# The second matrix product of the last pair of token tiles, by seven block products instead of eight

## The chip, the core and the metric

The kernel runs on one core of a Trainium2 chip. TensorE multiplies matrices into PSUM banks; VectorE and ScalarE do element-wise work; GpSimd has no part in what follows; SyncE (SP) issues the DMAs that move data between HBM and SBUF. Each engine works through its own queue in order and waits on semaphores. The metric is the device time of one execution in microseconds; lower is better.

## What is computed

```python
scores = scale * np.matmul(q, k.transpose(0, 1, 3, 2))     # 8 batches, 8 heads, 576 tokens, 64 dims
scores = np.where(masks[None], scores, -1e9)               # window 32, or 32 keys at a dilation of 4
attn = softmax(scores)
x = np.matmul(attn, v) -> (4608, 512)
h = x @ w_in                                               # (4608, 2048)
g = np.maximum(h, 0.0) + alpha * np.minimum(h, 0.0)
out = g @ w_out                                            # (4608, 512)
```

All in float32. On TensorE a float32 number is kept as two parts, a high one (a cast) and a low one (the number less its cast), and a product is three matmul passes: high by high, high weight by low data, low weight by high data (`PASSES`).

## The kernel before

There are 9 tiles of 512 tokens. The first three are worked one by one, mixed with most of the attention. Tiles 3 to 8 are worked as three pairs: (3, 4), (5, 6), (7, 8), in `paired_stage`. For each pair the hidden layer of 2048 is taken in two groups (`grp` 0 and 1) of four units; a unit is 256 hidden rows, two blocks of 128. Each group has two stages: `phase_h` (first product and activation) and `phase_y` (second product).

In `phase_h` the first product of a unit is already done by seven block products in place of eight (Strassen's scheme in Winograd's form). They are numbered 1 to 7, each is six matmuls of 512 columns, and their order for a unit is 1, then 3 and 4 of the unit before, then 7, 6, 2, 5. Bank A takes 1, 6, 5, 3 and is copied out after 1, 6 and 5 (`snap`, ScalarE, L646); banks B and C take 2, and 7 and 4, and are added to the copies (`add`, VectorE, L653). The four blocks of the hidden layer are called 11, 12, 21, 22: the first digit is the block of hidden rows, the second the token tile. For each, `negative` takes relu(-h) (ScalarE, L660), `value` builds the activation (VectorE, L664), `high` casts (ScalarE, L668) and `low` subtracts (VectorE, L672).

`phase_y` does the second product plainly: for each of four blocks `c` of 128 output features, eight blocks `j` of hidden rows, two token tiles and three passes, 192 matmuls (L742). Group 0 copies its sums to `partial` (L760, L762); group 1 adds them and stores the result (L765). Its steps are counted 8c + j, and `hooks` puts other work into all engines' queues at a step: the remaining attention pairs (five in the first stage, three, four and none in the next three; `scores`, `maxima`, `exponentials`, `divisions`, `turns`, `values`) and the splitting of the next pair's tokens (`token_parts`, L583 to L589). The last pair has neither.

The weights come back from HBM scratch (`wS`: seven blocks a unit for the first product, sums included; `wO`: plain split blocks for the second) through a ring of ten slots of 256 KB: `take` uses one, `feed` puts the next load on SP's queue. The buffers g1 to g4 hold the snapshots of `phase_h` and are free in `phase_y`.

The order of all instructions is written by hand; each engine's queue has them in program order.

Of the kernel before, what the change touches and what calls it, by code (L numbers as in the profile page):

```python
# [8 lines left out]
F32 = mybir.dt.float32  # L9
F32R = mybir.dt.float32r  # L10
# [7 lines left out]
P = 128  # L18
# [6 lines left out]
BK = 2 * BQ  # L25
# [35 lines left out]
def tile_window_attention_prelu_ffn(  # L61
# [31 lines left out]
    part = dram.tile([NC, P, TT], F32, name="part")  # L93
    wS = dram.tile([NFP, 7, P, 2, 2 * P], F32, name="wS")
    wO = dram.tile([NF // GF, NC, GP, P, 2, 2, P], F32, name="wO")

    turn = {"a": 0, "y": 0, "g": 0}

# [376 lines left out]


    WBLOCK = {1: 0, 2: 1, 4: 2, 3: 3, 7: 4, 5: 5, 6: 6}

    def save(f):

# [41 lines left out]
    PRODUCTS = (1, 7, 6, 2, 5, 3, 4)  # L522
    STEPS = [(i, q) for i in range(NFP) for q in PRODUCTS]
    units = []
    for _ in range(NSTD, NTILE, 2):
        for grp in range(NFP // GP):
            seq = []
            for i in range(GP):
                seq.append((i, 1))
                if i:  # L530
                    seq += [(i - 1, 3), (i - 1, 4)]
                seq += [(i, 7), (i, 6), (i, 2), (i, 5)]
            second = [wO[grp, c, j].rearrange("p f a n -> p (f a n)") for c in range(NC) for j in range(GP)]
            units += [wS[grp * GP + i, WBLOCK[q]].rearrange("p a n -> p (a n)") for i, q in seq]
            units.append(second[0])
            units += [wS[grp * GP + GP - 1, WBLOCK[q]].rearrange("p a n -> p (a n)") for q in (3, 4)]
            units += second[1:]
# [11 lines left out]

    def feed():  # L550
        if fed[0] < len(units):
            nc.sync.dma_start(out=slot(fed[0]).bitcast(F32), in_=units[fed[0]])
            fed[0] += 1

    def take():
# [120 lines left out]
            return gpart(2 * self.i + n // 20, n % 2 == 0)  # L676

    ABANKS = [f"a{i}" for i in range(4)]

    def third(u):  # L680
        u.mm(3)
# [15 lines left out]
        u.value(11)  # L697
        u.value(22)

    def phase_h(t, grp):  # L700

        last = None
        for i in range(GP):
            u = Four(t, grp, i)
            u.mm(1)
            u.snap(1)
            if last:
                after_first(last)
                third(last)
                fourth(last)  # L710
            u.mm(7)
            if last:
                last.low(22)
                last.low(12)
            u.mm(6)
            u.snap(2)
            if last:
                last.high(21)
            u.mm(2)
            u.add(11)  # L720
            if last:
                last.low(21)
            u.mm(5)
            u.snap(3)
            u.negative(11)
            u.add(22)
            last = u
        return last

    def phase_y(t, grp, u, hooks):  # L730

# [35 lines left out]
        for op in hooks.get(GF * NC, ()):  # L767
            op()

    def attention_hooks(hooks, us, start, step):  # L770
        def put(n, *ops):
            hooks.setdefault(min(n, GF * NC), []).extend(ops)
# [28 lines left out]
    def paired_stage():  # L801
# [4 lines left out]
        for t in range(NSTD, NTILE, 2):  # L806
            for grp in range(NFP // GP):
                hooks = {}
                last = phase_h(t, grp)
                if t == NSTD:  # L810
                    us, todo = (todo[:5], todo[5:]) if grp == 0 else (todo[:3], todo[3:])
                else:
                    us, todo = (todo[:4], todo[4:]) if grp == 0 else ([], todo)
                if us:
                    attention_hooks(hooks, us, *{5: (2, 5), 4: (3, 6), 3: (3, 5)}[len(us)])
                if grp and t + 2 < NTILE:
                    lots = token_parts(t + 2)
                    for at, lot in zip((7, 16, 22) if t == NSTD else (5, 11, 14), lots):
                        for k, op in enumerate(lot):
                            hooks.setdefault(at + k, []).append(op)  # L820
                phase_y(t, grp, last, hooks)

    late_ops = {}
# [321 lines left out]
```

## Time and profile before

| what | us |
|---|---|
| median of 3 runs | 876.26 |
| lowest and highest | 875.46, 878.27 |
| the profiled execution, its own time | 875.48 |
| span of the profiled execution, first to last instruction | 873.4 |
| TensorE busy in it | 845.0 |
| VectorE busy | 536.2 |
| ScalarE busy | 404.9 |

The span is what the profile's views divide up. In the rows, PE is TensorE, PEld its weight loads, DVE VectorE, ACT ScalarE, POOL GpSimd and SPq the DMA queue of SyncE; L742 is line 742 of the kernel; `out<-in` are the program's names for what an instruction writes and reads; "idle before <-X" is how long the engine stood before an instruction, and what ended the wait. [...]

### The profile page before, as it was taken

The numbers are of one execution on the slowest core, as the hardware profiler recorded it, in microseconds if no ns is written. First come the engines' busy times: TensorE is split into PE (matmuls) and PEld (weight loads), VectorE is DVE, ScalarE is ACT, GpSimd is POOL, SyncE is SP. The second block draws the span as 40 slices with busy tenths as digits, with TensorE's granted clock in tenths as the row PEclk, the third lists the DMA queues.
The fourth block names the chain that finished last, engine by engine and source line by source line (L and its number), as shares of the span: only waits on it lengthen the run. The fifth ranks groups of instructions, "written<-read, shape, count | busy, mean of one in ns | idle before, by whom it ended". The sixth has DMA issues, their size and how long they took to land.

```text
span 873.4 us, 19846 instructions
## 1 busy us (share of the span) xinstructions
PE 845.0 (97%) x8144; PEld 695.3 (80%) x8144; DVE 536.2 (61%) x924; ACT 404.9 (46%) x1153; POOL 46.9 (5%) x52
## 2 busy tenths in 40 slices
PE   4789999999999999999999999999999999999998
PEld 3577888888888788887788888887888888888886
DVE  5988767676776768675537665764277537304721
ACT  6785766534334344555436533643264226204500
POOL 0000000200505340000000000000000000000000
PEclk9789999999999999999999999999999999999999
DMA  9723344136889964765657666655475466336641
GB/s 337 250 72 121 121 163 145 41 103 203 275 283 317 283 211 127 254 184 162 186 166 193 186 178 192 193 153 157 127 193 151 150 188 192 114 96 178 183 122 48
DMA packets 95449, 152.81 MB, mean 175 GB/s; under 512 B 8448, under 2 KB 39168, under 8 KB 95360
## 3 DMA queue, kind: packets, MB, share of 16 engines
q1 hardware_dynamic: 95360, 151.55, 57.4%
q8 instruction: 64, 1.05, 0.5%
q14 instruction: 25, 0.20, 0.1%
HBM read 117.96 MB, written 33.55 MB: 173 GB/s over the span
## 4 chain that ended last, share of the span: by engine, by line
PE 95%; ACT 1%; issue 1%; DVE 1%; DMA 1%; SPq 0%
PE y L742 31%; PE h L406 16%; PE y L454 15%; PE pA L604 15%; PE pC L604 7%; PE pB L604 4%; PE o L279 3%; PE s L199 2%; PE o L230 1%; PE s L212 1%; DMA ws<-w_in 1%; ACT w_dt.float L249 1%; ACT wa L376 0%; ACT wa L375 0%; DVE x L338 0%
## 5 line engine op out<-in xcount | busy, mean ns | idle before, releaser
L406 PE MATMUL h<-x,w_dt.float32r 128*128 128x512 f32 x576 | 144.5, 400 | 2.9 <-issue 1.4
L454 PE MATMUL y<-g,w_dt.float32r 128*128 128x512 f32 x576 | 138.3, 389 | 0.0
L406 PEld LDWEIGHTS h<-x,w_dt.float32r 128*128 128x128 f32 x576 | 109.0, 192 | 26.9 <-issue 1.8
L454 PEld LDWEIGHTS y<-g,w_dt.float32r 128*128 128x128 f32 x576 | 107.9, 188 | 22.5
L742 PE MATMUL y<-gp,ring_w 128*128 128x512 f32 x480 | 113.6, 391 | 0.0
L249 ACT ACTIVATE pr<-pr,nm 128x64 f32<-128x64 f32 x216 | 72.2, 336 | 76.6 <-DVE nm L242 76.6
L742 PE MATMUL y<-gp,ring_xA 128*128 128x512 f32 x444 | 104.8, 391 | 0.0
L742 PEld LDWEIGHTS y<-gp,ring_w 128*128 128x128 f32 x480 | 89.4, 188 | 18.7
L742 PEld LDWEIGHTS y<-gp,ring_xA 128*128 128x128 f32 x444 | 82.7, 188 | 17.6
L646 ACT COPY stage<-pA 128x512 f32<-128x512 f32 x72 | 42.4, 589 | 105.0 <-PE pA L604 105.0
L432 ACT CAST g<-m 128x512 fp32r<-128x512 f32 x48 | 29.7, 619 | 75.6 <-DVE m L427 72.5
L672 DVE TENSOR_TENSOR gp<-n,gp 128x512 fp32r<-128x512 f32 x96 | 63.2, 684 | 0.0
L664 DVE SCALAR_TENSOR_TENSOR n<-n,bal,stage 128x512 f32<-128x512 f32 x72 | 53.9, 749 | 13.9 <-ACT n L660 13.1
L604 PE MATMUL pA<-parts_w,ring_w 128*128 128x512 f32 x234 | 57.6, 389 | 0.0
L668 ACT CAST gp<-n 128x512 fp32r<-128x512 f32 x96 | 56.6, 615 | 1.8 <-DVE n L664 1.8
L604 PE MATMUL pA<-parts_w,ring_xA 128*128 128x512 f32 x228 | 56.1, 389 | 0.0
L742 PE MATMUL y<-gp,ring_g 128*128 128x512 f32 x228 | 55.0, 393 | 0.0
L660 ACT ACTIVATE n<-stage 128x512 f32<-128x512 f32 x72 | 45.6, 634 | 12.5 <-DVE stage L653 12.0
L604 PEld LDWEIGHTS pA<-parts_w,ring_w 128*128 128x128 f32 x234 | 43.9, 188 | 9.1
L765 DVE TENSOR_TENSOR ob<-y,py 128x512 f32<-128x512 f32 x24 | 16.3, 689 | 54.9 <-PE y L742 54.9
L604 PEld LDWEIGHTS pA<-parts_w,ring_xA 128*128 128x128 f32 x228 | 42.8, 188 | 8.9
L742 PEld LDWEIGHTS y<-gp,ring_g 128*128 128x128 f32 x228 | 42.3, 188 | 9.0
(98 smaller groups left out, 1116.7 us busy)
## 6 DMA issues: line engine op xcount, KB each, us to landing
ring_w<-wS SPq DMA_DIRECT2D x68, 256.0 KB, 2.8
ring_xA<-wS SPq DMA_DIRECT2D x67, 256.0 KB, 2.8
ring_w<-wO SPq DMA_DIRECT2D x40, 256.0 KB, 2.9
ring_xA<-wO SPq DMA_DIRECT2D x37, 256.0 KB, 2.8
out<-ob SPq DMA_DIRECT2D x36, 256.0 KB, 2.9
ring_g<-wS SPq DMA_DIRECT2D x33, 256.0 KB, 3.0
wO<-w_dt.float32r SPq DMA_DIRECT2D x32, 256.0 KB, 4.8
wS<-wc SPq DMA_DIRECT2D x16, 512.0 KB, 3.9
```

The source lines that it names most:

```text
L249: nc.scalar.activation(out=self.pr[:, r, :], in_=self.pr[:, r, :], func=AF.Exp, bias=self.nm[:, r:r + 1], scale=1.0, accum_out=self.sm[:, ...
L279: nc.tensor.matmul(self.po[u][e * D:(e + 1) * D, a:z, :], lhsT=self.v[rows, i, :], rhs=self.pt[rows, a * BK + (BQ if i else 0):z * BK - (B ...
L406: nc.tensor.matmul(ms[t, f], lhsT=weight(0, a, f)[:, c * P:(c + 1) * P], rhs=half(t, c)[:, e, :], start=(c == 0 and n == 0), stop=(c == NC ...
L432: nc.scalar.copy(out=g[:, 0, :], in_=ms[t, f])
L454: nc.tensor.matmul(ys[t][c], lhsT=weight(1, a, f)[:, c * P:(c + 1) * P], rhs=g[:, e, :], start=(first and n == 0), stop=(last and n == 2),)
L604: nc.tensor.matmul(to, lhsT=w[:, (2 * a + c) * P:(2 * a + c + 1) * P], rhs=part_of(name, e)[:, c * TT:(c + 1) * TT], start=start and c == ...
L646: nc.scalar.copy(out=self.s(n), in_=self.A)
L660: nc.scalar.activation(out=self.m[n], in_=self.at(n), func=AF.Relu, scale=-1.0)
L664: nc.vector.scalar_tensor_tensor(out=self.m[n], in0=self.m[n], scalar=bal[:, f:f + 1], in1=self.at(n), op0=ALU.mult, op1=ALU.add)
L668: nc.scalar.copy(out=self.g(n)[:, 0], in_=self.m[n])
L672: nc.vector.tensor_tensor(out=g[:, 1], in0=self.m.pop(n), in1=g[:, 0].bitcast(F32), op=ALU.subtract)
L742: nc.tensor.matmul(ys2[tt], lhsT=w[:, k * P:(k + 1) * P], rhs=g[:, e], start=j == 0 and n == 0, stop=j == GF - 1 and n == 2)
```

## The change

The second product of the last pair is done by seven block products a unit too. A unit's hidden blocks 11, 12, 21, 22 are combined on VectorE to T1 = 12 - 11, T3 = 22 - 12, T2 = 22 - T1, T4 = 21 - T2, each split into a high and a low part; block 12 is needed only inside the terms and is not split. `seven_y` takes the place of `phase_y` for this pair: 28 products of six matmuls a group in the order `YSTEPS`, (unit, product), where (3, 0) stands for the first product's 3 and 4 of the fourth unit. The products of four units add up in three pairs of banks: A takes 1, 6, 5, 3, with a snapshot after each of the first three, B takes 2, C takes 7 and 4. In group 0 the snapshots are ScalarE copies, in group 1 VectorE adds onto group 0's. `BETWEEN` and `then` say where the terms and their splitting stand in the queues; whole blocks that a unit still needs are held in buffers that are free by then.

The seven products need four sums of weights for each unit (6, 7, 3 and 5 of `YBLOCK`). They are made once, in the `phase_y` stages of the earlier pairs, three units in the first of them, four in that of pair (5, 6)'s group 0, one in its group 1 (`second_sums`): four DMAs read the unit's blocks into g1 and g2 or g3 and g4, VectorE adds and subtracts, ScalarE casts, VectorE takes the low part, and two DMAs write the result to new scratch `wY`. `SUMS` gives for each unit the steps of the read, the sums and the split. The ring's list of loads for the last pair follows the new order; blocks from `wO` are then read as two runs of 1 KB a partition.

```diff
@@ -93,6 +93,7 @@
     wO = dram.tile([NF // GF, NC, GP, P, 2, 2, P], F32, name="wO")
+    wY = dram.tile([NFP, 4, P, 2, 2 * P], F32, name="wY")
@@ -475,6 +476,7 @@
     WBLOCK = {1: 0, 2: 1, 4: 2, 3: 3, 7: 4, 5: 5, 6: 6}
+    YBLOCK = {6: 0, 7: 1, 3: 2, 5: 3}
@@ -522,7 +524,10 @@
     units = []
-    for _ in range(NSTD, NTILE, 2):
+    YSTEPS = [(0, 1), (1, 1), (2, 1), (3, 0), (0, 2), (1, 2), (3, 1), (0, 7), (1, 7), (2, 7), (0, 6), (1, 6), (2, 6), (3, 7)]
+    YSTEPS += [(3, 6), (2, 2), (0, 5), (1, 5), (2, 5), (3, 5), (3, 2), (0, 3), (1, 3), (2, 3), (0, 4), (1, 4), (2, 4), (3, 4)]
+    YSTEPS += [(3, 3)]
+    for t in range(NSTD, NTILE, 2):
         for grp in range(NFP // GP):
@@ -530,8 +535,17 @@
                 seq += [(i, 7), (i, 6), (i, 2), (i, 5)]
+            units += [wS[grp * GP + i, WBLOCK[q]].rearrange("p a n -> p (a n)") for i, q in seq]
+            if t + 2 >= NTILE:
+                for i, q in YSTEPS:
+                    if q == 0:
+                        units += [wS[grp * GP + i, WBLOCK[q]].rearrange("p a n -> p (a n)") for q in (3, 4)]
+                    elif q in YBLOCK:
+                        units.append(wY[grp * GP + i, YBLOCK[q]].rearrange("p a n -> p (a n)"))
+                    else:
+                        units.append(wO[grp, 2 * (q == 4):2 * (q == 4) + 2, i, :, int(q != 1)].rearrange("c p a n -> p c (a n)"))
+                continue
             second = [wO[grp, c, j].rearrange("p f a n -> p (f a n)") for c in range(NC) for j in range(GP)]
-            units += [wS[grp * GP + i, WBLOCK[q]].rearrange("p a n -> p (a n)") for i, q in seq]
             units.append(second[0])
...
@@ -676,6 +691,52 @@
 ...
+    class Seven(Four):
+        HOLD = ({11: 0, 12: 1, 22: 2, 21: 3}, {11: 4, 12: 5, 22: 6, 21: 7}, {11: 0, 12: 1, 22: 2, 21: 8}, {11: 9, 12: 5, 22: 10, 21: 6})
+        PLACE = {11: (0, 1, 2, 3), 21: (4, 5, 6, 7), 22: (8, 9, 10, 11), "T2": (12, 13, 14, 15), "T3": (16, 17, 18, 19),
+                 "T1": (20, 21, 4, 5), "T4": (0, 1, 2, 3)}
+        TERMS = {"T1": (11, 12, 11), "T3": (12, 22, 12), "T2": (11, 22, 11), "T4": (21, 21, 11)}
+        def negative(self, n):
+            self.m[n] = hold(self.HOLD[self.i][n])
+            nc.scalar.activation(out=self.m[n], in_=self.at(n), func=AF.Relu, scale=-1.0)
+        def pair(self, name):
+            k = self.PLACE[name][self.i]
+            if k < 16:
+                return gts[k // 4][:, k % 4]
...
+        def whole(self, name):
+            return self.m[name if name in self.m else self.TERMS[name][0]]
+        def term(self, name):
+            out, x, y = self.TERMS[name]
+            nc.vector.tensor_tensor(out=self.m[out], in0=self.m[x], in1=self.m[y], op=ALU.subtract)
+        def high(self, n):
+            if n != 12:
+                nc.scalar.copy(out=self.pair(n)[:, 0], in_=self.whole(n))
+        def low(self, n):
+            if n != 12:
+                p = self.pair(n)
+                nc.vector.tensor_tensor(out=p[:, 1], in0=self.whole(n), in1=p[:, 0].bitcast(F32), op=ALU.subtract)
@@ -697,35 +758,48 @@
-    def phase_h(t, grp):
-
-        last = None
+    def phase_h(t, grp, kind=Four, between={}):
+        last, us = None, []
+        def more(at):
+            for k, op, name in between.get((i, at), ()):
+                getattr(us[k], op)(name)
+        stage.clear()
         for i in range(GP):
-            u = Four(t, grp, i)
+            u = kind(t, grp, i)
+            us.append(u)
             u.mm(1)
                 after_first(last)
+                more(1)
                 third(last)
+                more(3)
                 fourth(last)
                 last.low(12)
+            more(7)
             u.mm(6)
                 last.high(21)
+            more(6)
             u.mm(2)
                 last.low(21)
+            more(2)
             u.mm(5)
             u.add(22)
+            more(5)
             last = u
-        return last
+        return us
@@ -767,6 +841,156 @@
+    BETWEEN = {
+        (1, 7): [(0, "term", "T1"), (0, "term", "T3")],
+        (1, 6): [(0, "high", "T1"), (0, "high", "T3")],
+        (1, 2): [(0, "low", "T1")],
+        (1, 5): [(0, "low", "T3")],
+        (2, 1): [(0, "term", "T2"), (0, "high", "T2")],
+        (2, 7): [(0, "low", "T2"), (0, "term", "T4")],
+        (3, 1): [(1, "term", "T1"), (1, "high", "T1")],
+        (3, 7): [(1, "term", "T3"), (1, "low", "T1")],
+        (3, 6): [(1, "high", "T3")],
+        (3, 5): [(1, "low", "T3")],
+    }
+    def seven_y(t, grp, us):
...
+        tags = {"A": ("y0", "y1"), "B": ("y2", "y3"), "C": ("a2", "a3")}
+        banks = {}
+        def to(q):
+            name = {1: "A", 6: "A", 5: "A", 3: "A", 2: "B", 7: "C", 4: "C"}[q]
...
+        def snap(n):
+            for c in range(2):
+                if grp:
+                    nc.vector.tensor_tensor(out=out(n, c), in0=banks["A"][c], in1=out(n, c), op=ALU.add)
+                else:
+                    nc.scalar.copy(out=out(n, c), in_=banks["A"][c])
+        def add(n, name):
+            for c in range(2):
+                nc.vector.tensor_tensor(out=out(n, c), in0=banks[name][c], in1=out(n, c), op=ALU.add)
...
+        def then(step):
+            if step == (0, 1):
+                after_first(w0)
+                us[1].term("T2")
+                us[2].term("T1")
+                us[1].high("T2")
+                us[2].term("T3")
+                us[2].high("T3")
+            elif step == (1, 1):
+                us[1].low("T2")
+            elif step == (3, 0):
+                us[2].low("T3")
+            elif step == (0, 2):
+                w0.low(22)
+                w0.high(21)
+                us[2].high("T1")
+                w0.term("T1")
+                w0.term("T3")
+                w0.low(21)
+                w0.high("T3")
+            elif step == (1, 2):
+                w0.high("T1")
+                us[2].low("T1")
+                w0.low("T3")
+            elif step == (3, 1):
+                snap(11)
+                us[2].term("T2")
+                us[2].high("T2")
+                w0.low("T1")
+                w0.term("T2")
+                w0.high("T2")
+                us[2].low("T2")
+                us[1].term("T4")
+                w0.low("T2")
+                us[2].term("T4")
+                w0.term("T4")
+                for u in us:
+                    u.high("T4")
+            elif step == (3, 6):
+                snap(21)
+                for u in us:
+                    u.low("T4")
+            elif step == (3, 5):
+                snap(22)
+                add(22, "C")
+            elif step == (3, 2):
+                add(11, "B")
+            elif step == (3, 4):
+                add(21, "C")
+            elif step == (3, 3):
+                if grp:
+                    add(12, "A")
+                else:
+                    snap(12)
+        firsts = {(0, 1), (0, 2), (0, 7)}
+        names = {1: 11, 2: 21, 3: 22, 4: "T4", 5: "T1", 6: "T2", 7: "T3"}
+        for i, q in YSTEPS:
+            if q == 0:
+                third(w0)
+                fourth(w0)
+            else:
+                w, rhs = take(), us[i].pair(names[q])
+                for c in range(2):
+                    for n, (a, e) in enumerate(PASSES):
+                        k = 2 * a + c if q in YBLOCK else 2 * c + a
+                        nc.tensor.matmul(
+                            to(q)[c], lhsT=w[:, k * P:(k + 1) * P], rhs=rhs[:, e],
+                            start=(i, q) in firsts and n == 0, stop=i == GP - 1 and n == 2, skip_group_check=True)
+                feed()
+            then((i, q))
+    SUMS = {
+        (0, 0): ((0, 3, 8, 11, 1), (1, 12, 18, 21, 3), (2, 22, 27, 28, 1)),
+        (2, 0): ((3, 4, 10, 14, 1), (4, 10, 16, 20, 3), (5, 17, 22, 26, 1), (6, 23, 27, 29, 3)),
+        (2, 1): ((7, 18, 24, 27, 1),),
+    }
+    def second_sums(hooks, at):
+        for i, first, then, last, k in SUMS.get(at, ()):
+            room = {}
+            def fetch(i=i, k=k, room=room):
+                room["x"], room["t"] = (gbuf([P, 2, NC, P], F32, f"wy{i}_{a}", k + a) for a in range(2))
+                for a, x in enumerate((room["x"], room["t"])):
+                    for odd in range(2):
+                        nc.sync.dma_start(out=x[:, odd], in_=wO[i // GP, :, i % GP, :, odd, a].rearrange("c p n -> p c n"))
+            def sums(room=room):
+                x, t = (room[a].rearrange("p o c n -> p (o c n)") for a in "xt")
+                nc.vector.tensor_tensor(out=t, in0=x, in1=t, op=ALU.add)
+                t = t.rearrange("p (q n) -> p q n", q=4)
+                for out, x, y, op in ((3, 1, 3, ALU.add), (1, 0, 1, ALU.subtract), (0, 3, 0, ALU.subtract), (2, 2, 0, ALU.subtract)):
+                    nc.vector.tensor_tensor(out=t[:, out], in0=t[:, x], in1=t[:, y], op=op)
+            def parts(i=i, room=room):
+                x, t = (room[a].rearrange("p o c n -> p (o c n)") for a in "xt")
+                nc.scalar.copy(out=x.bitcast(F32R), in_=t)
+                nc.vector.tensor_tensor(out=t.bitcast(F32R), in0=t, in1=x, op=ALU.subtract)
+                for a, w in enumerate((x, t)):
+                    nc.sync.dma_start(
+                        out=wY[i, :, :, a].rearrange("q p n -> p q n"), in_=w.rearrange("p (q n) -> p q n", q=4))
+            for n, op in ((first, fetch), (then, sums), (last, parts)):
+                hooks.setdefault(n, []).append(op)
     def attention_hooks(hooks, us, start, step):
...
+                if t + 2 >= NTILE:
+                    seven_y(t, grp, phase_h(t, grp, Seven, BETWEEN))
+                    continue
+                last = phase_h(t, grp)[-1]
                 if t == NSTD:
@@ -818,6 +1045,7 @@
                             hooks.setdefault(at + k, []).append(op)
+                second_sums(hooks, (t - NSTD, grp))
                 phase_y(t, grp, last, hooks)
     late_ops = {}
```

## Rows read from the trace of the kernel before

**Rows 1.** The page's first part, TensorE: busy us, share of span, instructions.

```profile
PE 845.0 (97%) x8144; PEld 695.3 (80%) x8144; DVE 536.2 (61%) x924; ACT 404.9 (46%) x1153; POOL 46.9 (5%) x52
```

**Rows 2.** The chain of waits over the last pair: start us, us, what.

```profile
706.54 1.36 PE pA L604 x6
...
869.76 0.02 issue
869.78 0.69 DVE ob L765
```

**Rows 3.** Busy us of each engine by stage, granted clock, DMA share, GB/s.

```profile
242.00:264.00 22.00, 22.00 (x234) 17.98 (x232) 16.90 (x31) 7.12 (x26) 2.37 (x2) 1.00 0.92 294
286.00:308.00 22.00, 20.61 (x327) 16.70 (x329) 15.26 (x25) 8.21 (x26) 10.18 (x9) 1.00 0.90 281
395.00:443.00 48.00, 48.00 (x868) 38.27 (x869) 23.34 (x61) 19.35 (x109) 0.00 (x0) 1.00 0.61 170
569.00:625.00 56.00, 56.00 (x830) 45.06 (x829) 25.20 (x59) 21.70 (x101) 0.00 (x0) 1.00 0.50 142
706.50:747.30 40.80, 40.80 (x182) 33.78 (x181) 26.14 (x40) 22.46 (x41) 0.00 (x0) 1.00 0.69 195
747.30:788.00 40.70, 40.70 (x182) 33.68 (x181) 6.01 (x10) 4.44 (x8) 0.00 (x0) 1.00 0.37 103
```

**Rows 4.** VectorE in order of time in the last pair: start us, us, instruction.

```profile
726.31 0.75 DVE L664 SCALAR_TENSOR_TENSOR n<-n,bal,pA 128x512 f32<-128x512 f32 x1
726.98 0.69 DVE L653 TENSOR_TENSOR stage<-pC,stage 128x512 f32<-128x512 f32 x1
...
729.10 1.29 DVE L672 TENSOR_TENSOR gp<-n,gp 128x512 fp32r<-128x512 f32 x2
...
746.71 0.75 DVE L664 SCALAR_TENSOR_TENSOR n<-n,bal,pA 128x512 f32<-128x512 f32 x1 [2.01 <-ACT n L660]
```

**Rows 5.** VectorE's groups by shape, pairs' part: busy us, mean ns, idle before.

```profile
L672 DVE TENSOR_TENSOR gp<-n,gp 128x512 fp32r<-128x512 f32 x96 | 63.2, 684 | 0.0
L664 DVE SCALAR_TENSOR_TENSOR n<-n,bal,stage 128x512 f32<-128x512 f32 x72 | 53.9, 749 | 13.9 <-ACT n L660 13.1
...
L239 DVE SCALAR_TENSOR_TENSOR pr<-s,mask_sb 128x256 f32<-128x256 f32 x12 | 5.0, 415 | 0.0
L583 DVE TENSOR_TENSOR raw_xB<-raw_xB 128x1024 f32<-128x1024 f32 x3 | 3.7, 1222 | 0.0
```

**Rows 6.** ScalarE's groups by shape, the same part.

```profile
L668 ACT CAST gp<-n 128x512 fp32r<-128x512 f32 x96 | 56.6, 615 | 1.8 <-DVE n L664 1.8
```

**Rows 7.** VectorE in order of time in two second-product stages with attention.

```profile
437.16 0.78 DVE L264 STREAM_TRANSPOSE pt<-pr 128x576 f32<-128x576 f32 x1
...
588.84 0.42 DVE L242 TENSOR_REDUCE nm<-pr 128x4 f32<-128x256 f32 x1
591.46 0.52 DVE L340 COPY raw_xA<-o 128x160 f32<-128x160 f32 x2 [2.20 <-PE o L230]
...
593.14 0.78 DVE L264 STREAM_TRANSPOSE pt<-pr 128x576 f32<-128x576 f32 x1
```

**Rows 8.** The chain of waits at three places in those stages.

```profile
444.90 1.36 PE pA L604 x6
...
590.37 1.06 PE o L230 x56
...
600.94 1.05 PE o L230 x56
```

**Rows 9.** DMA issues of the page: count, KB each, median us to landing.

```profile
ring_w<-wO SPq DMA_DIRECT2D x40, 256.0 KB, 2.9
wO<-w_dt.float32r SPq DMA_DIRECT2D x32, 256.0 KB, 4.8
wS<-wc SPq DMA_DIRECT2D x16, 512.0 KB, 3.9
k<-kT SPq DMA_DIRECT2D x24, 288.0 KB, 3.9
```

**Rows 10.** What SP's queue waited for, pairs' part: us, times, longest us.

```profile
SPq L552 <- PE pA L604: 87.1, 92, 1.0
```

More of the change, by code (lines that the diff above doesn't have):

```diff
@@ L551, in feed @@
         if fed[0] < len(units):
-            nc.sync.dma_start(out=slot(fed[0]).bitcast(F32), in_=units[fed[0]])
+            to, u = slot(fed[0]).bitcast(F32), units[fed[0]]
+            nc.sync.dma_start(out=to if len(u.shape) == 2 else to.rearrange("p (c n) -> p c n", c=2), in_=u)
             fed[0] += 1
@@ L678, in tile_window_attention_prelu_ffn, with hold @@
     ABANKS = [f"a{i}" for i in range(4)]
+    held, split = [], {}
+    def hold(i):
+        if not held:
+            held.extend(ffp.tile([P, TT], F32, tag="m", name=f"held{k}", bufs=5) for k in range(5))
+            held.extend(att.tile([P, TT], F32, tag=tag, name=f"held_{tag}") for tag in ("k", "q", "v", "pt"))
+            held.extend(x[:, :TT // BK].rearrange("p j k -> p (j k)") for x in (pr0, mask_sb))
+        return held[i]
+    class Seven(Four):
[10 more added lines that the diff above has]
+                return gts[k // 4][:, k % 4]
+            tag = ("xB0", "xB1", "xA0")[(k - 16) // 2]
+            if tag not in split:
+                split[tag] = const.tile([P, 2, 2, TT], F32R, tag=tag, name=f"split_{tag}")
+            return split[tag][:, k % 2]
+        def whole(self, name):
[10 more added lines that the diff above has]
+                nc.vector.tensor_tensor(out=p[:, 1], in0=self.whole(n), in1=p[:, 0].bitcast(F32), op=ALU.subtract)
     def third(u):
@@ L768, in phase_y, with out @@
             op()
+    BETWEEN = {
[10 rows of a table added]
+    }
+    def seven_y(t, grp, us):
+        w0, end = us[3], grp + 1 == NFP // GP
+        tags = {"A": ("y0", "y1"), "B": ("y2", "y3"), "C": ("a2", "a3")}
+        banks = {}
+        def to(q):
+            name = {1: "A", 6: "A", 5: "A", 3: "A", 2: "B", 7: "C", 4: "C"}[q]
+            if name not in banks:
+                banks[name] = [psp.tile([P, TT], F32, tag=tag, name=f"q{name}{k}_{grp}") for k, tag in enumerate(tags[name])]
+            return banks[name]
+        def out(n, c):
+            return partial(2 * (n // 20) + c, int(n % 2 == 0))
+        def snap(n):
[7 more added lines that the diff above has]
+                nc.vector.tensor_tensor(out=out(n, c), in0=banks[name][c], in1=out(n, c), op=ALU.add)
+                if end:
+                    k, tt = 2 * (n // 20) + c, int(n % 2 == 0)
+                    nc.sync.dma_start(out=outT[k * P:(k + 1) * P, (t + tt) * TT:(t + tt + 1) * TT], in_=out(n, c))
+        def then(step):
[68 more added lines that the diff above has]
+            then((i, q))
```

1 line of the change is left out of this document (removed).

## The prediction

> **What bounds the kernel now.** Start with the page's first part: TensorE is busy 97% of the span [rows 1]. Busy alone does not say that it sets the end, so the second view is the chain of waits. From 706.54 us, where the last pair of tiles begins, to 869.76 us the chain is TensorE alone, without a piece of waiting [rows 2]: 163.22 us for 720 matmuls (168 and 192 for each half of the hidden layer, twice), or 0.2267 us each; a block product of six is 1.36 us. Then the stages [rows 3]: in the last pair's first-product stage VectorE is busy 26.14 of 40.80 us and ScalarE 22.46, in its second-product stage 6.01 and 4.44 of 40.70. The idle VectorE time that the change wants to use lies in the second kind of stage, and the DMA engines there have a share of 0.37. [...] Last, the single instructions that set the pace of VectorE and ScalarE [rows 4 to 6].
>
> **Fewer matmuls.** A unit (256 hidden rows, two token tiles) takes 2 x 4 x 2 x 3 = 48 matmuls in the second product now, and 7 x 6 = 42 after. Eight units: 48 matmuls less, 48 x 0.2267 = **10.88 us off**. They lie in the only queue of the chain, so all of it counts unless TensorE is made to wait.
>
> **VectorE in the last pair.** A unit has 11 VectorE operations now (4 values, 3 adds, 4 lows). After it has 18 (block 12 needs no split, so 3 lows; 4 terms, 4 lows of terms). The page of groups gives 684 ns for a low and 749 for a value [rows 5], but records overlap: two lows in a row last 1.29 us, so the second starts 0.61 us after the first, and the add starts 0.67 us after the value [rows 4]. A term reads and writes SBUF; its nearest row is the 1024-wide difference (1222 ns, the same per element as a low of that width), so I give it a low's price. A group of four units is 56 x 0.61 + 16 x 0.67 = 44.9 us in 56 products x 1.36 = 76.2 us. On the mean that fits; what decides is bunching. In the second to fourth units 13 or 14 operations fall on 9.52 us (8.2 to 8.8 us of pitches), and the value of block 12 waits for ScalarE in between, as it does now for 2.01 us at worst [rows 4].
>
> I laid both queues out operation by operation with these pitches, 0.52 us for a cast and the like on ScalarE (its record is 615 ns, [rows 6]) and 0.04 us from an end to its waiter. VectorE runs without a gap worth the name from the second product of the third unit until the lows of T4. The tightest place can be checked by count. In the second group the snapshot after (3, 1) is an add on VectorE, and (0, 6) must not write its banks before it. From product 2 of the third unit to (0, 6) there are 19 products, 25.84 us. In that time VectorE has 34 operations (8 values) and the snapshot: 26 x 0.61 + 8 x 0.67 + 0.73 = 21.95 us. It starts 1.72 us behind and waits 2.75 us for ScalarE in all, 26.4 us; with 0.19 us that TensorE itself lost before, 0.4 us late. The other late places are product 2 of the fourth unit in both groups (0.19 us each, the add that frees its bank stands behind the term T1 of the unit before and ScalarE's cast of it) and (2, 6) in the second group (0.22 us). Sum 1.0 us. In the first group the snapshots are ScalarE's and wait for nobody.
>
> The bounds: nothing, if pitches are 0.04 us shorter, and 8.7 us, if every operation held VectorE for its whole record. The same layout with 0.02 us more per operation gives 2.4 us, so the queue has no reserve. The measured 0.61 is nearest; I take **1.5 us lost**, a little above the layout.
>
> [...]
>
> **Weight sums in the earlier pairs.** Eight units are summed, three in the first second-product stage, four in that of pair (5, 6), one in the next. Each has one 1024-wide addition, four 256-wide and one 1024-wide low on VectorE, one 1024-wide cast on ScalarE. The trace has no 256-wide SBUF addition; bounds are 0.35 us (half a low) and 0.42 us (a 256-wide operation from PSUM, [rows 5]). I take the latter: 1.22 + 4 x 0.42 = 2.9 us for the sums, 1.22 for the low. Cover: in pair (5, 6)'s stage VectorE is busy 25.20 of 56 us and gets 16.5 more; in the first stage 23.34 of 48 and gets 12.4 [rows 3]. The sums stand behind a pair's maxima. These end at 589.26 us, the next copy starts at 591.46 [rows 7], so 2.2 of 2.9 us are idle now and 0.7 us push that copy (raw tokens, wanted much later) and the division behind it. The transpose ends at 593.92 and the values that read it start on TensorE at 600.94 [rows 7, 8]: 7 us of slack. Cost nothing; with that cover gone 0.7 us a time.
>
> DMA: a unit reads 1 MB and writes 1 MB. For four, 8.4 MB in 56 us, or 150 GB/s on top of 142 [rows 3], 292. The stage that saves weights in runs of 512 bytes carried 294 GB/s at a share of 0.92 with TensorE full, and 281 with 1.39 us of 22 lost [rows 3]. Bounds: nothing, and 1.39 x 56 / 22 = 3.5 us a stage. The sums' read is issued four to seven steps of 1.36 us ahead; under load 256 KB in such runs landed in 4.8 us [rows 9]. I take **0.3 us**.
>
> On SP's queue the reads stand behind the release of buffers g1 to g4, and the writes behind VectorE's low. Behind them wait ring loads and the attention's q, k and v. A ring load has ten units of lead, 13.6 us at the fast pace. The first snapshot of the next first product writes g1, from which a weight write may still be reading. In the first stage the fifth pair's transpose ends at 437.94 us [rows 7]; 2.9 us of sums and a cast of at most 1.2 (two of 615 ns) put that write at 442.0, and it lands 3.9 us later [rows 9], at 445.9. The snapshot is due at 446.26, when the first product there ends [rows 8]. Nothing, barely.
>
> **The ring in the last pair.** It now takes 256 KB per 1.36 us (193 GB/s) for the whole pair. The first-product stage does that already at a share of 0.69 [rows 3], with SP always the one that waits, at most 1.0 us [rows 10]. Twelve of 28 units come in 1 KB runs instead of 2 KB: from the 2.9 us that a load lands in to at most the 4.8 us of half such runs, against 12 us of lead. Nothing.
>
> **The end.** Now 0.69 us of VectorE follow the last matmul. After, two adds of (3, 4) run until about 1.4 us into the last product and two of (3, 3) follow: 0.9 us. **0.2 us lost.**
>
> **Sum.** -10.88 + 1.5 + 0.3 + 0.2 = -8.9 us. The profiled execution took 875.48 us (span 873.4 and 2.1 around it) and would take 866.6; the median of the runs shown is 0.78 above it, so 876.26 - 8.9 = **867.4 us**. About 0.3%, 2.6 us, is what a measurement of this kernel can tell from no change.
>
> **Rivals.** A is the forecast, 865.4 (no stall) to 870. *B: VectorE becomes the bound.* If an operation holds the engine for its whole record, TensorE waits 8.7 us and 0.5 is lost elsewhere: 874.6 us, within what can be told from none. For it: the queue without reserve. Against it: starts 0.61 us apart. *C: the weight reads come late.* VectorE stands in order at the first sum until its data is there, the division behind it is late, and TensorE waits for the values. For it: 292 GB/s. Against it: 7 us of slack. At the upper bound of 3.5 us, 870.6 us. *D, the other side: SP's queue.* A weight write waits on SP for VectorE's low, and the next pair's q and k stand behind it, so TensorE waits at the scores. Nine attention pairs lie in the two stages with seven of the sums; the kernel gets slower by over 0.3% once each loses (8.9 + 2.6) / 9 = 1.3 us. q and k are issued a pair ahead (two value stages are 10.57 us apart, from the chain's 590.37 to 600.94 us) and land in about 4 [rows 8, 9], so SP would have to be held over 7 us at a time. The low stands at most some 4 us behind its step. At 2 us each, 876.26 - 8.9 + 18 = 885 us.
>
> **How the numbers follow.** A 0.79, B 0.07, C 0.10, D 0.04. The time is A's. The range starts below A's best by the spread of the runs shown, 864.8, and reaches over C to 872.0; B and D, 0.11, lie above. Faster: A and C, 0.89. Same: B, 0.07. Slower: D, 0.04.
>
> **What would show it.** The profile after should have 8096 matmuls; from the last pair's start to the last matmul 153 to 155 us; VectorE almost gapless from its third unit to the lows of T4; waits of TensorE before product 2 of the fourth unit and before (0, 6) of the second group, a few tenths each. Before 706 us nothing should move. Waits of the value matmuls or scores in the stages with sums would prove C or D; VectorE starts 0.69 us apart would prove B. I am wrong if either the last pair gains less than 7 us or the earlier stages lose over 2.

## The result, and the profile after

The changed kernel takes 868.6 us (median of 6 runs, 865.99 to 869.0) against 877.14 us of the kernel before beside it (6 runs): a ratio of 0.9897, 95% interval 0.9878 to 0.9917. That is 8.5 us less; 8.9 were forecast, and 868.6 lies in the range given. In a later measurement the same two kernels stood 6.8 us apart (868.78 against 875.57, last row of the table below). The profiled execution took 868.86 us with a span of 866.7.

The page's first part shows the 48 matmuls less, and VectorE at 606 us in place of 536 [rows 1]:

```profile
span 866.7 us, 20071 instructions
...
PE 836.1 (96%) x8096; PEld 686.2 (79%) x8096; DVE 606.0 (70%) x1036; ACT 429.2 (50%) x1189; POOL 46.9 (5%) x52
```

Busy time by stage (columns as in [rows 3]): the two second-product stages that got three and four units' sums, then the first group of the last pair, first and second product.

```profile
393.00:446.00 53.00, 52.81 (x960) 41.90 (x959) 37.29 (x83) 24.78 (x120) 0.00 (x0) 1.00 0.82 256
579.00:628.40 49.40, 48.00 (x794) 38.52 (x794) 34.81 (x74) 20.87 (x97) 0.00 (x0) 1.00 0.91 283
710.00:745.60 35.60, 35.60 (x158) 29.16 (x157) 26.04 (x41) 20.54 (x37) 0.00 (x0) 1.00 0.73 205
745.60:786.40 40.80, 40.80 (x182) 33.78 (x181) 24.64 (x40) 15.19 (x27) 0.00 (x0) 1.00 0.71 193
```

TensorE stays full in the last pair and lost 1.40 us in the stage of pair (5, 6). What TensorE waited for from the pairs' first matmul on (us in total, times, longest):

```profile
PE y L816 <- issue: 1.4, 1, 1.4
PE pA L619 <- ACT stage L661: 0.4, 1, 0.4
PE o L231 <- DMA v<-vX: 0.2, 1, 0.2
```

"Issue" says that the engine waited for nothing that the profile shows; this one is called the stop below. And its weight loads in the last pair alone:

```profile
PEld pB L619 <- DVE stage L668: 0.9, 4, 0.3
PEld qA L952 <- DVE gp L739: 0.3, 1, 0.3
PEld qA L952 <- DVE py L875: 0.2, 1, 0.2
```

The places named before are among them: product 2 of the fourth unit in both groups (pB, behind VectorE's add), and product 6 of the first and of the third unit in the second group, behind the snapshot (L875) and a low (L739). Product 2 of the third unit, 0.17 us in each group, was not named; it is the other two of the four pB waits.

In what follows two stretches of each trace are compared: *first*, from the start of the pairs' first block product to the start of the last pair, and *last*, from there to the end of the last matmul. Before: 355.28 and 163.36 us. After: 358.18 and 153.21 us. So the last pair gained 10.15 us, and the earlier pairs, where no matmul changed, lost 2.90: 7.25 us less by these two traces. In the table below one execution is left out of the median, one of 1052.8 us of the kernel with ScalarE's queue, in which the granted clock was 0.75.

### The profile page after: what moved, and what is told of

Read it like the earlier page. It is cut to its first block, busy times and chain, and to the rows that moved or that the text cites. A ratio compares the mean times of both kernels' runs of the same rounds, so it can differ in the third digit from the quotient of the medians.

```text
span 866.7 us, 20071 instructions
## 1 busy us (share of the span) xinstructions
PE 836.1 (96%) x8096; PEld 686.2 (79%) x8096; DVE 606.0 (70%) x1036; ACT 429.2 (50%) x1189; POOL 46.9 (5%) x52
## 3 DMA queue, kind: packets, MB, share of 16 engines
q8 instruction: 64, 1.05, 0.5%
## 4 chain that ended last, share of the span: by engine, by line
PE 93%; DMA 2%; ACT 2%; DVE 2%; issue 1%; SPq 0%; ACTq 0%
PE y L816 20%; PE h L407 16%; PE y L455 15%; PE pA L619 15%; PE pC L619 7%; PE qA L952 5%; PE pB L619 4%; PE o L280 3%; PE qC L952 2%; PE s L200 2%; PE o L231 1%; PE qB L952 1%; PE s L213 1%; DMA ws<-w_in 1%; ACT w_dt.float L250 1%
## 5 line engine op out<-in xcount | busy, mean ns | idle before, releaser
L816 PE MATMUL y<-gp,ring_w 128*128 128x512 f32 x324 | 77.7, 393 | 0.0
L816 PE MATMUL y<-gp,ring_xA 128*128 128x512 f32 x300 | 71.7, 393 | 0.0
L816 PEld LDWEIGHTS y<-gp,ring_w 128*128 128x128 f32 x324 | 60.1, 188 | 12.8
L816 PEld LDWEIGHTS y<-gp,ring_xA 128*128 128x128 f32 x300 | 55.7, 188 | 12.2
L668 DVE TENSOR_TENSOR stage<-pC,stage 128x512 f32<-128x512 f32 x48 | 33.1, 690 | 16.1 <-ACT stage L661 15.9
L438 DVE TENSOR_TENSOR g<-m,g 128x512 fp32r<-128x512 f32 x48 | 33.6, 701 | 15.1 <-ACT g L433 15.0
L679 DVE SCALAR_TENSOR_TENSOR n<-n,bal,stage 128x512 f32<-128x512 f32 x48 | 35.9, 749 | 9.2 <-ACT n L675 8.7
L687 DVE TENSOR_TENSOR gp<-n,gp 128x512 fp32r<-128x512 f32 x64 | 42.1, 684 | 0.0
L427 DVE TENSOR_SCALAR m<-h,al 128x512 f32<-128x512 f32 x27 | 20.2, 748 | 29.5 <-PE h L407 29.4
L250 ACT ACTIVATION_READ_ACCUMULATOR pr<-pr,nm 128x1 f32 x216 | 40.8, 189 | 0.0
```

Source lines behind the costliest of these rows:

```text
L250: nc.scalar.activation(out=self.pr[:, r, :], in_=self.pr[:, r, :], func=AF.Exp, bias=self.nm[:, r:r + 1], scale=1.0, accum_out=self.sm[:, ...
L438: nc.vector.tensor_tensor(out=g[:, 1, :], in0=ms.pop((t, f)), in1=g[:, 0, :].bitcast(F32), op=ALU.subtract)
L668: nc.vector.tensor_tensor(out=self.s(n), in0=getattr(self, src), in1=self.s(to), op=ALU.add)
L679: nc.vector.scalar_tensor_tensor(out=self.m[n], in0=self.m[n], scalar=bal[:, f:f + 1], in1=self.at(n), op0=ALU.mult, op1=ALU.add)
L687: nc.vector.tensor_tensor(out=g[:, 1], in0=self.m.pop(n), in1=g[:, 0].bitcast(F32), op=ALU.subtract)
L816: nc.tensor.matmul(ys2[tt], lhsT=w[:, k * P:(k + 1) * P], rhs=g[:, e], start=j == 0 and n == 0, stop=j == GF - 1 and n == 2)
```

## Experiments

Theory: the 2.9 us are the weight sums' (their transfers, or their VectorE work), and in the last pair it is the order in VectorE's queue that TensorE waits for. Rivals: the loss is the spread of executions; or VectorE takes up any work in the last pair. The stretches of all runs, in us, with the ratio to the kernel before, measured beside it, and its interval:

| kernel | first | last | median | ratio |
|---|---|---|---|---|
| before | 355.28 | 163.36 | | |
| changed | 358.18 | 153.21 | 868.6 | 0.9897 (0.9878 to 0.9917) |
| no sums | 355.76 | 153.13 | 867.24 | 0.9896 (0.9878 to 0.9914) |
| sums only | 359.14 | 163.36 | 879.84 | 1.0034 (1.0021 to 1.0047) |
| sums spread | 359.24 | 155.00 | 871.29 | 0.9940 (0.9926 to 0.9954) |
| a low twice | 357.72 | 158.06 | 873.3 | 0.9961 (0.9946 to 0.9976) |
| ScalarE's queue | 365.12 | 153.17 | 876.47 | 1.0009 (0.9995 to 1.0024) |
| sums apart | 355.60 | 153.14 | 866.68 | 0.9892 (0.9874 to 0.9910) |
| last pair's order | 357.46 | 152.62 | 868.75 | 0.9915 (0.9898 to 0.9932) |
| DMAs alone | 357.36 | 153.14 | 868.1 | 0.9914 (0.9897 to 0.9930) |
| both | 355.60 | 152.56 | 865.75 | 0.9891 (0.9873 to 0.9910) |
| changed, again | 357.77 | 153.18 | 868.78 | 0.9931 (0.9912 to 0.9951) |

Each stretch is from one trace. Four of these kernels have the same first stretch (changed, a low twice, last pair's order, changed again); it took 357.46 to 358.18 us in them, so a difference of some 0.7 us between two rows shows nothing by itself.

**No sums.**

```diff
-                        units.append(wY[grp * GP + i, YBLOCK[q]].rearrange("p a n -> p (a n)"))
+                        units.append(wS[grp * GP + i, WBLOCK[q]].rearrange("p a n -> p (a n)"))
...
-                second_sums(hooks, (t - NSTD, grp))
```

> The last pair's second product by seven block products, without the weight sums in the earlier pairs (the last pair reads blocks of the first product's weights of the same size in their place, so the output is not the reference's). Theory 1, the sums cost time: the changed kernel's trace lost 0.44 and 0.83 us in the two stages around the first three sums' end, where a snapshot waits for a weight write, and 1.63 us in pair (5, 6), where TensorE stood 1.40 us for instructions while the DMA engines had a share of 0.91; without the sums these go and the kernel is 1.3 to 2.9 us faster than the changed one, 10.0 to 11.3 us faster than before, a ratio of 0.987 to 0.9885. The last pair alone stays at 153.1 us. Rival, the losses are the spread of executions: the ratio stays at 0.990, and stretches of the same length are lost elsewhere.

The first stretch falls by 2.42 us and TensorE's three waits in it are gone, as expected. With the matmuls of the two traces matched one by one, the changed kernel falls behind in three steps: 0.26 us at the wait for v, 0.55 at the snapshot, 1.47 at the stop. The ratio, 0.9896, did not move: it misses the expected 0.987 to 0.9885, though its interval reaches into them. So the trace speaks for the sums' cost, and the ratios of two separate measurements cannot tell 2.4 us; the last pair of experiments was therefore put side by side.

**Sums only.**

```diff
-            if t + 2 >= NTILE:
+            if False:
                 for i, q in YSTEPS:
...
-                if t + 2 >= NTILE:
-                    seven_y(t, grp, phase_h(t, grp, Seven, BETWEEN))
-                    continue
```

> The kernel before with the weight sums alone, their result unused. Theory 1: 1.3 to 2.9 us slower than before, a ratio of 1.0015 to 1.0033, with the same wait of the snapshot at the start of the second group of pair (3, 4). Prediction on record: 0.3 us, a ratio of 1.0003, which this can hardly tell from 1. Rival D of the prediction (SP's queue held) would give waits of TensorE at the scores and several us.

3.3 us slower by the medians, 3.86 by the first stretch, more than the 1.3 to 2.9 expected, and here the ratio does tell it from 1: the sums cost, and the 0.3 us on record was wrong. The snapshot's wait did not come in this execution; two waits for v did, 1.8 us in all, beside the same stop of 1.4 us. In SP's queue (start us, us):

```profile
412.00 2.82 SPq L988 DMA_DIRECT2D wY<-wy  x2
414.93 1.58 SPq L178 DMA_DIRECT2D k<-kT  x1
416.56 0.45 SPq L179 DMA_DIRECT2D q<-qT  x1
417.06 2.08 SPq L974 DMA_DIRECT2D wy<-wO  x4
419.24 2.01 SPq L567 DMA_DIRECT2D ring_xA<-wS  x2
421.35 0.38 SPq L186 DMA_DIRECT2D v<-vX  x1
```

From the second weight write (414.46 us) to v, SP issues without a pause. These issues take 0.37 to 1.58 us each; the median issue in the trace before takes 0.32, though single ones there take as much as 1.72. The v load landed 6.32 us after its issue, and the value matmuls waited for it.

**Sums spread.**

```diff
-        (0, 0): ((0, 3, 8, 11, 1), (1, 12, 18, 21, 3), (2, 22, 27, 28, 1)),
-        (2, 0): ((3, 4, 10, 14, 1), (4, 10, 16, 20, 3), (5, 17, 22, 26, 1), (6, 23, 27, 29, 3)),
-        (2, 1): ((7, 18, 24, 27, 1),),
+        (0, 0): ((0, 3, 8, 11, 1), (1, 12, 18, 21, 3)),
+        (0, 1): ((2, 4, 9, 13, 1),),
+        (2, 0): ((3, 4, 10, 14, 1), (4, 10, 16, 20, 3)),
+        (2, 1): ((5, 3, 9, 11, 1), (6, 8, 14, 18, 3), (7, 18, 24, 27, 1)),
```

> The changed kernel with the sums placed otherwise: two units in the first second-product stage, one in the next, two in that of pair (5, 6), three in its second group, and none that ends in the last steps of a stage with attention. Theory 1: the snapshot's wait for the weight write goes and the DMA share in the stage of pair (5, 6) falls from 0.91 to some 0.7, so the kernel gains 0.8 to 2.5 us over the changed one, a ratio to before of 0.987 to 0.989. Rival, spread of executions: 0.990.

A miss: 2.7 us slower than the changed kernel by the medians. The 1.4 us in pair (5, 6) are gone, but in the stage that got one unit a v load left SP late (517.39 us) and TensorE waited 1.7 us; and VectorE stood 2.44 us for the last unit's reads, so that unit's write to scratch, out of g1, was issued at 709.92 us, 1.3 us before the last pair began (in the changed kernel it left at 705.10, 4.8 us before). The last pair's first snapshot waited for it:

```profile
PE o L231 <- DMA v<-vX: 1.7, 1, 1.7
PE pA L619 <- ACT stage L661: 1.5, 1, 1.5
```

```profile
705.70 1.23 DVE L979 TENSOR_TENSOR wy<-wy,wy 128x1024 f32<-128x1024 f32 x1 [2.44 <-DMA wy<-wO]
```

So fewer sums in a stage were not enough: where their reads and writes stand still cost 3 us.

**A low twice.**

```diff
                 p = self.pair(n)
-                nc.vector.tensor_tensor(out=p[:, 1], in0=self.whole(n), in1=p[:, 0].bitcast(F32), op=ALU.subtract)
+                for _ in range(2 if n == "T3" else 1):
+                    nc.vector.tensor_tensor(out=p[:, 1], in0=self.whole(n), in1=p[:, 0].bitcast(F32), op=ALU.subtract)
```

> The changed kernel with the low part of T3 taken twice in each unit of the last pair: one VectorE operation of 0.68 us more a unit, four a group, same output. Theory V, VectorE's queue has no reserve in the last pair: laid out with the same pitches, TensorE's waits in the last pair go from 1.0 to 6.2 us, so the last pair takes about 158 us in place of 153.1, the kernel is 5 us slower than the changed one, a ratio to before of 0.995 to 0.997; the longest single wait, about 2.1 us, is before product 6 of the first unit in the second group. Rival, the idle 14 us of VectorE in each group take it up: the last pair stays at 153 to 154 us and the ratio at 0.990.

Eight operations of 0.68 us cost 4.85 us in the last pair, 158.06 us as laid out. TensorE's waits in it:

```profile
PE qA L953 <- DVE py L876: 1.7, 1, 1.7
PE pB L619 <- DVE stage L668: 0.9, 2, 0.4
PE qA L953 <- ACT py L878: 0.2, 1, 0.2
```

The longest is the snapshot before (0, 6), as expected. VectorE's queue has no reserve there, though in the changed kernel VectorE is busy only 26.04 of 35.60 and 24.64 of 40.80 us: its idle time comes later, where it is of no use. Two stretches of the changed kernel's first group (VectorE's busy time is the third of the five):

```profile
750.00:760.00 10.00, 10.00 (x46) 8.29 (x45) 9.24 (x16) 6.58 (x12) 0.00 (x0) 1.00 0.70 198
770.00:780.00 10.00, 10.00 (x46) 8.28 (x45) 2.57 (x4) 1.18 (x2) 0.00 (x0) 1.00 0.74 193
```

**ScalarE's queue.** In `second_sums`:

```diff
-                        nc.sync.dma_start(out=x[:, odd], in_=wO[i // GP, :, i % GP, :, odd, a].rearrange("c p n -> p c n"))
+                        nc.scalar.dma_start(out=x[:, odd], in_=wO[i // GP, :, i % GP, :, odd, a].rearrange("c p n -> p c n"))
...
-                    nc.sync.dma_start(
+                    nc.scalar.dma_start(
                         out=wY[i, :, :, a].rearrange("q p n -> p q n"), in_=w.rearrange("p (q n) -> p q n", q=4))
```

> The changed kernel with the six DMAs of each unit's sums issued from ScalarE's queue instead of SP's. Theory S, SP's queue is what costs: with the sums alone two v loads left SP 3.5 and 5.1 us after their turn, behind weight writes and reads, and TensorE waited 1.1 us for one; with another queue no value matmul waits for v, and the first two pairs' stages come within 0.5 us of those without the sums, so the kernel gains 1 us or more. Theory B, the DMA engines' load is what costs: the 1.4 us without instructions in pair (5, 6), at a DMA share of 0.92 to 0.99, stays, and so does the wait of the snapshot for the weight write (0.4 us and more); the ratio to before stays at 0.990.

No value matmul waits for v now, which speaks for theory S, but the whole gain is lost: ScalarE works in order too. In the first stage it stood 6.7 us before the third unit's cast, and the tokens' last copies, which the next first product reads, came after it:

```profile
PE pA L619 <- ACT raw_xB L334: 4.5, 1, 4.5
```

The stop without a wait shrank to 0.5 us, where theory B expected it to stay at 1.4. S and B are not told apart by this run, since it made a longer wait of its own.

**DMAs alone.** `sums` does nothing and `parts` only writes:

```diff
-                nc.scalar.copy(out=x.bitcast(F32R), in_=t)
-                nc.vector.tensor_tensor(out=t.bitcast(F32R), in0=t, in1=x, op=ALU.subtract)
```

> The changed kernel with the DMAs of the weight sums but without their VectorE and ScalarE work (unsummed weights are written, so the output is not the reference's). Theory B or S: the loss before the last pair stays, 2 us or more against the kernel without sums (358 us from the first block product to the last pair), with the 1.4 us in pair (5, 6). Rival, VectorE's 33 us of sums delay the attention: the loss goes, 355.8 us.

Of the 2.42 us, 1.60 stay with the transfers alone, less than the 2 expected: against the kernel without sums, TensorE falls behind by 1.48 us at the stop and 0.58 at a v load. The snapshot does not wait here, so the 0.55 us at it belong to the sums' work on VectorE and ScalarE; the rest of the difference is within what two traces differ by. The stop goes with the load on the DMA engines. For 612.50 to 616.50 us, where it falls, the changed kernel (TensorE 2.60 of 4.00 us, DMA share 1.06):

```profile
612.50:616.50 4.00, 2.60 (x91) 2.00 (x90) 3.39 (x9) 3.73 (x21) 0.00 (x0) 1.00 1.06 355
```

DMAs alone:

```profile
612.50:616.50 4.00, 2.59 (x39) 2.10 (x26) 3.08 (x9) 1.56 (x10) 0.00 (x0) 1.00 0.97 335
```

No sums:

```profile
612.50:616.50 4.00, 4.00 (x81) 3.39 (x68) 3.09 (x9) 1.95 (x12) 0.00 (x0) 1.00 0.54 160
```

**Sums apart.** Reads stand behind a load of v, not ahead of it; no stage ends with a split in g1 and g2.

```diff
-        (0, 0): ((0, 3, 8, 11, 1), (1, 12, 18, 21, 3), (2, 22, 27, 28, 1)),
-        (2, 0): ((3, 4, 10, 14, 1), (4, 10, 16, 20, 3), (5, 17, 22, 26, 1), (6, 23, 27, 29, 3)),
-        (2, 1): ((7, 18, 24, 27, 1),),
+        (0, 0): ((0, 3, 8, 11, 1), (1, 16, 23, 26, 3)),
+        (2, 0): ((2, 4, 10, 14, 3), (3, 12, 18, 21, 1), (4, 18, 24, 27, 3)),
+        (2, 1): ((5, 2, 7, 9, 1), (6, 5, 10, 12, 3), (7, 11, 14, 17, 1)),
```

> The changed kernel with two units' sums in the first second-product stage, three in that of pair (5, 6) and three in its second group, no reads in the step before a load of v, and none that ends at a stage's end in g1 and g2. Theory B and S both: from 706 us back the kernel runs as without sums, to within 0.5 us (355.8 us from the first block product to the last pair in place of 358.2), so it gains 1.5 to 2.5 us over the changed one, a ratio to before of 0.987 to 0.988. If some v load or a snapshot still waits, the trace names it and the gain is that much less. Rival, spread of executions: 0.990.

The first stretch takes 355.60 us with all eight sums in it, 0.16 less than without any. So the sums' cost is a matter of how they are placed. This run changes two things in the stage of pair (5, 6), the steps and the number of units (three instead of four); which of them took the stop away it does not tell. The median ratio, 0.9892, falls short of the expected 0.987 to 0.988, which its interval reaches.

**The last pair's order.**

```diff
-        (3, 1): [(1, "term", "T1"), (1, "high", "T1")],
-        (3, 7): [(1, "term", "T3"), (1, "low", "T1")],
-        (3, 6): [(1, "high", "T3")],
+        (3, 7): [(1, "term", "T1"), (1, "term", "T3")],
+        (3, 6): [(1, "high", "T1"), (1, "high", "T3")],
+        (3, 2): [(1, "low", "T1")],
...
-                w0.low("T3")
             elif step == (3, 1):
                 snap(11)
+                w0.low("T3")
```

> The changed kernel with five operations of the last pair moved: the term and cast of T1 of the second unit behind the first product's 3 and 4, its low behind product 2, and the low of T3 of the fourth unit behind the first snapshot. Theory V, these orders are what TensorE waits for: the same layout gives no wait in place of 1.0 us, the last pair takes 152.4 us to the last matmul's issue instead of 153.1, 0.7 us or 0.1% less, which the trace shows and the ratio can hardly. Rival, VectorE is short of time as such: the waits move to other products and the last pair stays at 153.1 us or grows.

152.62 us: 0.59 of the 0.73 us that the last pair lost (worked out below) come back with the same number of operations. One kind of wait is left there, at product 2 of the third unit:

```profile
PEld pB L619 <- DVE stage L668: 0.3, 2, 0.2
```

**Both, beside the changed kernel.**

> The moved sums and the moved operations of the last pair together. If the two losses add up as the traces say (2.6 us between the first block product and the last pair, 0.6 us in the last pair), these stretches take 355.6 and 152.6 us, and the kernel is some 3 us faster than the changed one beside it on the same chip, a ratio to before of 0.986 to 0.988. If what the traces showed is the spread of executions, the two do not differ by more than 1 us.

> The changed kernel as it is, beside the one above, for a comparison on one chip. Its first stretch again takes about 358 us, with 1.4 us in pair (5, 6) and a snapshot waiting for a weight write, and the last pair 153.2 us; a ratio to before of 0.990.

865.75 against 868.78 us on one chip, 3.0 us less, and the intervals of the two ratios do not meet. The losses add up as the traces say: 355.60 and 152.56 us against 357.77 and 153.18. Both ratios came out 0.001 to 0.003 higher than expected (0.9891 for 0.986 to 0.988, 0.9931 for 0.990). This version beats both kernels.

## Why the prediction was right, and where not

The time came out in the range, but by the prediction's own sign ("the earlier stages lose over 2") its account of the earlier pairs failed: they lost 2.90 us.

*Fewer matmuls, 10.88 us.* Right. 672 matmuls at 0.2267 us are 152.34 us. The last stretch before, 163.36 us, is 0.14 longer than its 720 matmuls at that price, so 152.48 us is the last stretch after without a wait.

*VectorE in the last pair, 1.5 us.* The mechanism was right, the size too large: 153.21 - 152.48 = 0.73 us, and the layout by pitches had said 1.0, with four of the six places. The allowance of 0.5 on top of it was not needed. Terms cost what a low costs, and operations follow each other 0.60 to 0.61 us apart (start us, us):

```profile
743.86 0.68 DVE L739 TENSOR_TENSOR gp<-held,gp 128x512 fp32r<-128x512 f32 x1
744.46 0.68 DVE L730 TENSOR_TENSOR held_k<-held_q,held_k 128x512 f32<-128x512 f32 x1
745.07 0.68 DVE L739 TENSOR_TENSOR split_xA<-held,split_xA 128x512 fp32r<-128x512 f32 x1
```

This refutes rival B, by which an operation holds the engine for its whole record: each of these starts 0.07 to 0.08 us before the end of the record ahead of it. That there was no reserve was right too, as the doubled low showed.

*Weight sums, 0.3 us.* This is the step that failed: the prediction took "0.3 us" for the transfers and "Nothing, barely" for the snapshot. They cost 2.42 us by the two traces compared, 1.7 to 2.4 by the four with this first stretch; the upper bound was 3.5. The prices were right (a 256-wide operation 425 ns, 420 assumed; 283 GB/s in pair (5, 6)'s stage, 292 forecast). Three things were wrong. First, the third unit's reads came late. SP took 3.31 us to issue the four, and each landed up to 6.1 us after its issue (5.7 in the median of all, not 4.8); the last landed at 440.89. So VectorE stood 2.38 us before the third unit's sum (the row names a ring load that was landing in the same microsecond), which is rival C's stand but not its path: it did not go by the division, it pushed the write out of g1 past the snapshot:

```profile
432.61 3.31 SPq L974 DMA_DIRECT2D wy<-wO  x4
...
441.12 1.23 DVE L978 TENSOR_TENSOR wy<-wy,wy 128x1024 f32<-128x1024 f32 x1 [2.38 <-DMA ring_g<-wS]
...
445.29 1.63 SPq L988 DMA_DIRECT2D wY<-wy  x2
...
448.45 0.58 ACT L661 COPY stage<-pA 128x512 f32<-128x512 f32 x1 [2.28 <-DMA wY<-wy]
```

The write was forecast for 442.0 us and was issued at 445.29, 3.3 late; the 0.55 us that TensorE lost at the snapshot are "barely" gone wrong. Some 0.6 us of the 3.3 are the later start of the whole stretch (351.70 us, not 351.10). Next, rival D counted q and k behind the weight DMAs on SP's queue but not v, which is issued only when its buffer is free and so has the least time to land: the queue was right, the load was not the one named. Last, the stop of 1.4 us, the largest of the three losses, was in none of the steps as what it is. The prediction had one like it in hand: the 1.39 us lost of 22 [rows 3], which it spread over the stage as 1.39 x 56 / 22, is a single stop of the same kind in the trace before.

```profile
295.87 2.35 PE L406 MATMUL h<-x,w_dt.float32r 128*128 128x512 f32 x9 [1.39 <-issue]
```

*The end, 0.2 us.* Nothing: the last add ends 0.73 us after the last matmul in both traces (863.82 after 863.09, and 870.47 after 869.74), since VectorE had done with (3, 4) in time.

*The ring in the last pair, nothing.* Right: no load of it was waited for at 193 GB/s.

That the forecast came out 0.4 us from the measured difference is luck. With the terms as measured the sum is -10.88 + 0.73 + 2.42 = -7.7 us, and the two traces say 7.25; terms too large by 0.8 and 0.2 and one too small by 2.1 cancel in part, and medians move: that of the kernel before was 875.47 to 877.14 us in the four measurements, and the same two kernels stood 8.5 us apart in one and 6.8 in another. The range's lower end, 864.8, is not what its words give (865.4 less 0.8 is 864.6); nothing hangs on it.

## What to carry to other kernels

Before adding transfers to a stage, walk the queue that issues them and find the load with the least time to land, not the one with the longest way; put the new reads behind it and never just ahead of it, and let no buffer of the next stage be the source of a late write. An engine's idle share need not be its reserve (here VectorE was busy 50.68 of 76.40 us in the last pair's first group, and eight operations of 0.68 us more in the pair cost 4.85 us): lay its queue out operation by operation with start-to-start times, and see where its consumers stand. If the same sums cost 2.4 us in one placing and nothing in another, the placing is the thing to tune. And before a row with a loss is scaled to a longer stage, see whether the loss is a rate or one event.

## What the runs showed of the hardware

TensorE stood 1.2 to 1.4 us for nothing that the profile's waits show, at the same matmul, behind the third attention pair's value matmuls, in the six traces that have four units' transfers in the stage of pair (5, 6) on SP's queue (changed, again, sums only, a low twice, last pair's order, DMAs alone), and 0.5 us with ScalarE's queue. It did so in none of the five others, with three units or fewer there (before, no sums, sums spread, sums apart, both).

The records of single DMA packets in the traces before and after show what ended last there. Beside the kernel's own DMAs there are reads of instructions; the page after lists them so (queue, kind: reads, MB, share of the DMA engines):

```profile
q8 instruction: 64, 1.05, 0.5%
```

These 64 reads of 16 KB are taken here to be TensorE's, an estimate: they are some four fifths of the instruction bytes in that part of the page (1.05 of 1.28 MB), and TensorE with its weight loads has four fifths of the trace's instructions (16192 of 20071). In the changed kernel's trace the 54th of them lasts from 613.49 to 614.37 us, and the matmul after the stop starts at 615.98, 1.61 us after its end. In the trace before, the 54th ends at 610.05 us, and the same matmul starts at 612.56, 2.51 us later and without a stop. The stop near 296 us is in both traces (1.39 us before, 1.1 us in the changed kernel's); it ends 1.50 and 1.31 us after the end of the 27th such read (294.37 and 295.16 us). In the stretch of 4 us around the later stop the DMA engines' share was 1.06 (changed) and 0.97 (DMAs alone), and 0.54 without sums, where TensorE did not stop. More than that these times lie close together is not shown: no run changes when the instructions are read and nothing else. "For instructions", as the expectation of *no sums* puts it, is its author's reading of 1.40 us that the trace has as "issue".

An SP issue takes 0.32 us in the median in the trace before, from 345 to 712 us, and 0.33 in the changed kernel's. Of 235 issues before, 22 take over 0.4 us, the longest 1.72; of 280 in the changed kernel 68, the longest 1.99. Long issues can make a load late: in *sums only* v left SP at 421.35 us, behind the issues shown there, and the value matmuls waited for it. They need not: in the trace before TensorE is busy 367.00 of the 367.00 us from 345 to 712.

The part ahead of the pairs, the same instructions in all twelve traces, ended between 350.26 and 353.59 us. So two spans can lie 3.33 us apart for that part alone, and a smaller difference between them is read here from a stretch in which it arises, or from runs on one chip side by side.
